# One row of the second weight chunk turned to columns on TensorE instead of through DRAM, and the first even part moved between the two halves of the sine ring's update, with a later conversion of the third weight chunk

## The chip, the cores and the metric

The kernel runs on one core of a Trainium2 chip. The metric is the device time of one execution in microseconds (us). I quote medians over executions with their extremes. The calls ran on different chips (chip 15, 14, 7 and 3), each timed one with the kernel before in the same rounds; medians of different calls are therefore compared with care.

## The reference

```python
def reference(x, w_in, w_out):            # x: 8 x 3008 x 256, w_in: 256 x 2048, w_out: 2048 x 256
    X = np.fft.fft(np.fft.fft(x, axis=1), axis=2).real.astype(np.float32)
    h = X.reshape(-1, 256) @ w_in
    g = np.where(h > 0.0, h, np.exp(np.minimum(h, 0.0)) - 1.0)
    return (g @ w_out).astype(np.float32)
```

The weights arrive as 64-bit floats. The kernel converts them with integer operations, chunk by chunk, while the main work is already running.

## The kernel before

The kernel works in steps, each on 256 sequence positions. The sequence transform gives rings of cosine rows (`Rr`) and sine rows (`Ir`); the channel transform is folded into the first weights, which gives `Wc` and `Ws`. In a step, a cosine product P = `Rr` by `Wc` and a sine product Q = `Ir` by `Ws` are made on TensorE. By symmetry h = E - Q for one half of the positions and E + Q for the other, with the even part E = P + (channel 128) x (its weights).

Channel 128 is the odd one out of 256. Its weights of chunk c are the row 127 of `Ws`, and VectorE needs them as *columns* `wex`, one number for each partition (the cuts of code leave out wrappers, and `...` marks left-out lines):

```python
def even_part(i):
    ...
    for j in range(2):
        f = 2 * (i % 8) + j
        c = slice(j * TW, (j + 1) * TW)
        nc.vector.scalar_tensor_tensor(out=S.E[:, c], in0=Rb[:, cols(i)],
            scalar=wex[:, f : f + 1], in1=S.H[:, c], op0=ALU.mult, op1=ALU.add)

def spread_last_row(q):                      # row 127 of Ws to columns, by way of DRAM
    c = slice(q * 256, (q + 1) * 256)
    queue = nc.sync if q else nc.gpsimd
    queue.dma_start(out=wx_dr[:, c], in_=Ws[127:128, c])
    queue.dma_start(out=wex[:, 2 * q : 2 * q + 2],
                    in_=wx_dr[:, c].rearrange("o (f p) -> p (o f)", p=128))
```

A weight chunk is converted by two masks on VectorE (`fields`), three ScalarE operations (`power`), a GpSimd sum (`round`), and a VectorE sign operation followed by a GpSimd product (`scale`); then TensorE folds it (`fold_chunk`), and ScalarE puts it into `Ws` and `Wc` (`put_chunk`).

The *cosine transform of channel 128 of the later batches* is made at step 25 from an extra input: a gather of single 4-byte elements of x, in sixteen pieces, to SBUF, to DRAM and back in another layout. I call these "the extra channel's rows":

```python
at((13 + 0.7 * n) * T, lambda j=j, k=k: load_ext(j, 192 * k, 192 * (k + 1)))   # n = 0 .. 15
at(24.4 * T, get_ext)                         # read back from DRAM
at(25 * T + 1.35, fold_ext)                   # GpSimd
at(25 * T + 4.75, dft_ext)                    # TensorE
```

`at(t, ...)` puts work at a place in the order of the program; `T` is a step. It sets order, not time.

## Time and profile before

| | us |
|---|---|
| median of the first three runs (lowest, highest) | 1979.97 (1978.64, 1984.95) |
| span of the traced execution | 1978.7 |
| TensorE busy | 1960.0 |
| TensorE waiting for E at Q0, Q1, Q2 | 1.45, 0.84, 4.39 |
| P0 starts; P3 starts; P3 to the end | 27.50; 53.88; 1924.81 |

How to read it: what is not TensorE's own work is found in its waits, and nearly all of them lie in the first 60 us. So three marks are enough: when the first cosine product P0 starts, how long P0 to P3 takes (the stretch that the change touches), and how long P3 to the end takes. The prediction shows the lines themselves.

### The profile page before, as it was taken

The numbers are of one execution on the slowest core, as the hardware profiler recorded it, in microseconds if no ns is written. First come the engines' busy times: TensorE is split into PE (matmuls) and PEld (weight loads), VectorE is DVE, ScalarE is ACT, GpSimd is POOL, SyncE is SP. The second block draws the span as 40 slices with busy tenths as digits, with TensorE's granted clock in tenths as the row PEclk, the third lists the DMA queues.
The fourth block names the chain that finished last, engine by engine and source line by source line (L and its number), as shares of the span: only waits on it lengthen the run. The fifth ranks groups of instructions, "written<-read, shape, count | busy, mean of one in ns | idle before, by whom it ended". The sixth has DMA issues, their size and how long they took to land.

```text
span 1978.7 us, 26821 instructions
## 1 busy us (share of the span) xinstructions
PE 1960.0 (99%) x8896; PEld 1665.0 (84%) x8896; DVE 1273.9 (64%) x2322; ACT 869.4 (44%) x1666; POOL 1333.9 (67%) x1804
## 2 busy tenths in 40 slices
PE   8999999999999999999999999999999999999998
PEld 4888888888888888888888888888888888888887
DVE  7766656666566666666566665666556765666665
ACT  3554434444444444444444443444444444344443
POOL 3388748776577766777567775678657776455655
PEclk9999999999999999999999999999999999999999
DMA  9146201121001110011100211003010110100101
GB/s 355 32 20 45 80 15 19 31 62 22 14 19 43 46 29 12 18 50 41 26 18 13 64 26 26 11 19 89 7 21 12 20 22 14 16 12 12 22 10 23
DMA packets 255740, 71.08 MB, mean 36 GB/s; under 512 B 244255, under 2 KB 245044, under 8 KB 255090
## 3 DMA queue, kind: packets, MB, share of 16 engines
q1 hardware_dynamic: 251026, 56.53, 14.8%
q0 software_dynamic: 2400, 12.59, 1.9%
q8 instruction: 70, 1.15, 0.2%
q14 instruction: 68, 0.56, 0.1%
q10 hardware_dynamic: 2176, 0.26, 0.1%
HBM read 44.50 MB, written 24.80 MB: 35 GB/s over the span
## 4 chain that ended last, share of the span: by engine, by line
PE 96%; DVE 1%; DMA 1%; POOL 1%; issue 0%; ACT 0%; POOLq 0%; DVEq 0%; ACTq 0%
PE H L350 39%; PE pD L350 16%; PE pB L350 16%; PE pC L350 16%; PE pA L350 8%; DMA xl<-in_x_dram,ix 1%; DMA wx<-Ws 0%; DVE E L710 0%; DMA wex<-wx 0%; POOL G L359 0%; DVE v L356 0%; DVE e L423 0%; DVE o L423 0%; DVE Ir L356 0%; DVE G L736 0%
## 5 line engine op out<-in xcount | busy, mean ns | idle before, releaser
L359 POOL TENSOR_TENSOR G<-G 128x256 f32<-128x256 f32 x1440 | 1036.8, 729 | 564.8 <-DVE G L736 453.3
L710 DVE SCALAR_TENSOR_TENSOR E<-Rb,wex,H 128x256 f32<-128x256 f32 x752 | 327.9, 477 | 621.4 <-PE H L350 614.1
L362 ACT ACTIVATE G<-H 128x512 f32<-128x512 f32 x376 | 224.6, 597 | 960.6 <-DVE G L720 960.6
L350 PE MATMUL H<-Ir,Ws 128*128 128x256 f32 x1504 | 388.2, 381 | 6.7 <-DVE E L710 6.7
L350 PE MATMUL H<-Rr,Wc 128*128 128x256 f32 x1504 | 386.4, 379 | 0.0
L350 PE MATMUL pC<-G,WT 128*128 128x256 f32 x1440 | 369.5, 379 | 0.0
L350 PEld LDWEIGHTS H<-Rr,Wc 128*128 128x128 f32 x1504 | 285.1, 190 | 53.8 <-issue 2.5
L350 PEld LDWEIGHTS H<-Ir,Ws 128*128 128x128 f32 x1504 | 278.1, 189 | 56.2 <-DVE E L710 8.9
L350 PEld LDWEIGHTS pC<-G,WT 128*128 128x128 f32 x1440 | 273.6, 190 | 37.2
L720 DVE SCALAR_TENSOR_TENSOR G<-E,H 128x512 f32<-128x512 f32 x376 | 257.3, 684 | 37.5 <-PE H L350 1.9
L736 DVE SCALAR_TENSOR_TENSOR G<-G,H 128x512 f32<-128x512 f32 x376 | 256.0, 681 | 24.9 <-ACT G L362 24.8
L736 DVE SCALAR_TENSOR_TENSOR G<-M,G 128x512 f32<-128x512 f32 x376 | 257.2, 684 | 0.0
L362 ACT ACTIVATE G<-G 128x512 f32<-128x512 f32 x376 | 233.2, 620 | 0.0
L350 PE MATMUL pB<-G,w 128*128 128x256 f32 x784 | 231.0, 382 | 0.0
L350 PE MATMUL pA<-G,w 128*128 128x256 f32 x784 | 229.4, 379 | 0.2 <-POOL w L359 0.2
L350 PE MATMUL pD<-G,w 128*128 128x256 f32 x784 | 229.3, 379 | 0.0
L362 ACT ACTIVATE M<-G 128x512 f32<-128x512 f32 x376 | 224.0, 596 | 0.0
L362 ACT ACTIVATE M<-M 128x512 f32<-128x512 f32 x376 | 221.0, 588 | 0.0
L350 PE MATMUL pD<-G,WT 128*128 128x256 f32 x720 | 214.4, 379 | 1.6 <-DVE v L356 1.6
L350 PE MATMUL pB<-G,WT 128*128 128x256 f32 x720 | 214.5, 379 | 0.5 <-POOL G L359 0.5
L350 PEld LDWEIGHTS pB<-G,w 128*128 128x128 f32 x784 | 150.1, 192 | 20.8
L350 PEld LDWEIGHTS pA<-G,w 128*128 128x128 f32 x784 | 148.9, 190 | 20.8 <-POOL w L359 0.6
(127 smaller groups left out, 1382.9 us busy)
## 6 DMA issues: line engine op xcount, KB each, us to landing
out_dram<-ot SPq DMA_DIRECT2D x496, 32.0 KB
xl<-in_x_dram SPq DMA_DIRECT2D x16, 768.0 KB
MC<-dft_mats SPq DMA_DIRECT2D x4, 1131.0 KB
out_dram<-ot SPq DMA_DIRECT2D x256, 2.0 KB
Rb<-r SPq DMA_DIRECT2D x10, 376.0 KB
raw<-in_moe_w_in_dram SPq DMA_DIRECT2D x7, 512.0 KB
raw<-in_moe_w_out_dram SPq DMA_DIRECT2D x5, 512.0 KB
out_dram<-ot SPq DMA_DIRECT2D x64, 28.0 KB
```

Of the source, the lines that this page charges most:

```text
L350: nc.tensor.matmul(out_, lhsT=lhsT, rhs=rhs, start=start, stop=stop, skip_group_check=True)
L359: pin(nc.gpsimd.tensor_tensor(out=o, in0=a, in1=b, op=op))
L362: pin(nc.scalar.activation(out=o, in_=i, func=func, **kw))
L710: nc.vector.scalar_tensor_tensor(out=S.E[:, c], in0=Rb[:, cols(i)], scalar=wex[:, f : f + 1], in1=S.H[:, c], op0=ALU.mult, op1=ALU.add,)
L720: nc.vector.scalar_tensor_tensor(out=two(S.G[:, 0:512])[:, :, ::-1], in0=two(S.E), scalar=2.0, in1=two(S.H), op0=ALU.mult, op1=ALU.subtract,)
L736: nc.vector.scalar_tensor_tensor(out=o, in0=e, scalar=-1.0, in1=h, op0=ALU.add, op1=ALU.max)
```

## The change

The intent: Q2 waits 4.39 us for two DMA hops of 1 KB. Two TensorE products of one column each can do the same. With a stationary operand of 128 columns of `Ws` and a moving operand that is 1 in row 127 and 0 elsewhere, the product is row 127 as a column. ScalarE copies it to `wex`. Besides, E0 goes between the two updates of the sine ring, and the conversion of chunk 2 moves later, so that VectorE is free for E1.

```diff
-    m = np.zeros((128, 32), np.float32)
+    m = np.zeros((128, 33), np.float32)
     m[np.arange(128), np.arange(128) % 32] = 1.0
+    m[127, 32] = 1.0
...
-    pick = cpool.tile([128, 32], FP, tag="pick")
+    pick = cpool.tile([128, 33], FP, tag="pick")
...
+    def turn_last_row(q):
+        for j in range(2):
+            f = 2 * q + j
+            mm(folds[q][:, j : j + 1], Ws[:, f * 128 : (f + 1) * 128], pick[:, 32:33], True)
+
+    def put_last_row(q):
+        act(wex[:, 2 * q : 2 * q + 2], folds[q][:, 0:2])
...
     w1_chunks[1].load()
+    nc.sync.dma_start(out=pick, in_=PK_dr.ap())
...
-    at(1.2, lambda: nc.sync.dma_start(out=pick, in_=PK_dr.ap()))
...
-        at(t - 0.5 if k else 0.95, chunk.fields)
-        at(t + 0.05 if k else 0.96, chunk.power)
-        at(t + 0.06 if k else 0.97, chunk.round)
-        at(t + 2.95 if k else 1.9, chunk.scale)
+        at(0.96 if k == 0 else t + 3.0 if k == 1 else t - 0.5, chunk.fields)
+        at(0.96 if k == 0 else t + 3.05 if k == 1 else t + 0.05, chunk.power)
+        at(0.97 if k == 0 else t + 3.06 if k == 1 else t + 0.06, chunk.round)
+        at(1.9 if k == 0 else t + 4.22 if k == 1 else t + 2.95, chunk.scale)
...
-        at(t + 0.01, lambda c=c: spread_last_row(c))
+        if c > 1:
+            at(t + 0.01, lambda c=c: spread_last_row(c))
+    at(T + 0.2, lambda: turn_last_row(1))
+    at(T + 0.25, lambda: put_last_row(1))
...
-        (0.1, I_even.minus),
+        (0.95, I_even.minus),
```

(Here k = 1 and 2 are the places of the chunks 2 and 3 of the first weights; k = 0 is the first chunk of the second weights. Chunk 1 was converted before. `pick` is the moving operand of the turn, its column 32 new.)

More of the change, by code (lines that the diff above doesn't have):

```diff
@@ L394, in spread_last_row @@
             )
+    def turn_last_row(q):
+        for j in range(2):
+            f = 2 * q + j
+            mm(
+                folds[q][:, j : j + 1],
+                Ws[:, f * 128 : (f + 1) * 128],
+                pick[:, 32:33],
+                True,
+            )
+    def put_last_row(q):
+        act(wex[:, 2 * q : 2 * q + 2], folds[q][:, 0:2])
     w2v = w2.rearrange("p (q c) -> p q c", c=ND)
@@ L969, in mid_pick @@
         po = state["mo"] = bank("H")
-        mm(po[0:32, 0:ND], pick, state["mh"][:, 0:ND], True)
+        mm(po[0:32, 0:ND], pick[:, 0:32], state["mh"][:, 0:ND], True)
     def mid_store():
```

## The prediction

> **What bounds the kernel now.** I read the page first: busy shares, the chain of waits, the costliest groups. Then the waits of TensorE alone, then the chain in order of time over the first 60 us, and last the timelines of TensorE, VectorE and GpSimd over 27 to 57 us.
>
> ```profile
> PE 1960.0 (99%) x8896; PEld 1665.0 (84%) x8896; DVE 1273.9 (64%) x2322; ACT 869.4 (44%) x1666; POOL 1333.9 (67%) x1804
> PE 96%; DVE 1%; DMA 1%; POOL 1%; issue 0%; ACT 0%; POOLq 0%; DVEq 0%; ACTq 0%
> ```
>
> TensorE sets the time nearly everywhere: 99% busy, 96% of the chain. What is not TensorE's work can only be found in its waits, which are few:
>
> ```profile
> PE H L350 <- DVE E L710: 6.7, 3, 4.4
> PE pD L350 <- DVE v L356: 1.6, 3, 0.5
> PE M L350 <- DVE zero L337: 1.1, 1, 1.1
> PE pC L350 <- DMA MC<-dft_mats: 0.8, 1, 0.8
> PE pB L350 <- POOL G L359: 0.5, 1, 0.5
> ```
>
> The columns are the total in us, the number, and the longest. Three waits of the sine product for the even part E make 6.7 us of some 11. All are early, as TensorE's timeline shows (start, length, work, idle before it):
>
> ```profile
> 29.98 1.10 PE L350 MATMUL H<-Ir,Ws 128*128 128x256 f32 x4 [1.45 <-DVE E L710]
> 36.41 1.13 PE L350 MATMUL H<-Ir,Ws 128*128 128x256 f32 x4 [0.84 <-DVE E L710]
> 40.13 1.89 PE L350 MATMUL pA<-G,w 128*128 128x256 f32 x8
> 46.41 2.07 PE L350 MATMUL H<-Ir,Ws 128*128 128x256 f32 x4 [4.39 <-DVE E L710]
> 48.28 3.62 PE L350 MATMUL pB<-G,w 128*128 128x256 f32 x8
> 51.69 2.36 PE L350 MATMUL H<-w,CC 128*128 128x256 f32 x8
> 53.88 1.03 PE L350 MATMUL H<-Rr,Wc 128*128 128x256 f32 x4
> ```
>
> I call these sine products Q0, Q1, Q2 (step 0, 1, 2), the cosine products before them P0, P1, P2, P3, and the even parts E0, E1, E2. After Q2's wait eight matmuls of 128x256 take 3.62 us; just before it, 1.89. The busy table by stretch shows why, in its clock column (PEclk, before the DMA share): half speed after the wait.
>
> ```profile
> 46.40:51.70 5.30, 5.29 (x13) 4.21 (x14) 4.28 (x7) 2.12 (x4) 1.27 (x1) 0.50 0.47 168
> 54.00:58.00 4.00, 4.00 (x21) 3.51 (x20) 3.05 (x5) 2.35 (x5) 1.30 (x1) 1.00 0.04 3
> ```
>
> What Q2 waited for stands in the chain in order of time: the 1 KB row 127 of Ws, written to DRAM and read back as columns.
>
> ```profile
> 33.25 6.83 DMA wx<-Ws
> 40.09 5.29 DMA wex<-wx
> 45.88 0.49 DVE E L710
> ```
>
> The data is tiny; the hops are long because bulk loads are in flight. The DMA engines are at 90% or more of each slice until about 45 us.
>
> **What the Trainium skill says.** (1) "TensorE: Matmul & The Clock Gate", Part 1: the gate knows half and full speed, falls to half after an idle window of about 3.4 us and needs about as long a busy one to come back. The trace agrees: an idle 4.39 us was followed by clock 0.50 for some 5 us, the idle 1.45 us at Q0 by none. (2) The same page, LDWEIGHTS (loading the stationary operand): a weight load costs by its columns, about 107 ns for 128. The trace differs: its fp32 loads of 128x128 take 190 ns, and a product has two. They are hidden beside matmuls of 256 columns (216 ns from start to start); beside matmuls of one column they are not, so the turn costs its loads. (3) "SBUF — State Buffer", Who interferes with whom: VectorE in a two-port mode, or with two SBUF inputs, and GpSimd exclude each other for a whole instruction. The trace agrees, and this decides my size below: the integer mask ops of a weight chunk take 0.41 us alone and far more beside GpSimd:
>
> ```profile
> 32.98 1.18 DVE L211 TENSOR_SCALAR pow<-raw 128x512 int32<-128x512 int32 x1
> 34.08 1.49 DVE L217 TENSOR_SCALAR w<-raw 128x512 int32<-128x512 int32 x1
> 33.95 1.34 POOL L359 TENSOR_TENSOR w<-w,pow 128x512 f32<-128x512 f32 x1
> ```
>
> The second mask stood right behind the first and still had to let the GpSimd product pass, which had asked earlier. (4) "DMA: Bandwidth & Descriptors", Issuing engines are not separate DMA queues: all issuers share the same 16 engines. It fits the 12 us of the two hops; another queue would not have helped.
>
> **The change part by part.** The built order differs on few places: on TensorE two one-column products (turn) behind P1; on VectorE E0 between the two Ir instructions, chunk 2's masks behind g of step 0, its sign/exponent op behind the two Rr instructions of the odd DFT; on ScalarE one 128x2 copy; two row DMAs gone. GpSimd's order is unchanged. I walk it through with durations of the trace; durations overlap by some 0.08 us on VectorE, so I use starts.
>
> 1. *E0 first.* E0 started 28.96, after both Ir instructions (28.04 and 28.51). Behind the first alone it starts 28.49, ends 29.36, and Q0 goes 0.15 later, 29.52 instead of 29.98. The next work, the fold of chunk 1, needs GpSimd's 29.10 + 1.27 = 30.37, so it starts 30.47 instead of 30.91: gain 0.44. Risk: row 0's columns, by the GpSimd queue, land at 20.98 + 6.6 = 27.6, still 0.9 early.
>
> 2. *The turn.* P1 then ends its turn on TensorE at 30.47 + 1.73 + 0.87 = 33.07. The turn waits for the put of chunk 1 (ScalarE, ends about 33.1): four loads, 4 x 0.19 = 0.76, the following DFT's first load no longer hidden, 0.19, and the wait, 0.07: 1.0 us. The DFT starts 34.1 and Q1 36.0.
>
> 3. *Q1's wait goes.* E1 stood behind the two masks (32.98 to 35.57) and started 35.49. Now it follows h of step 0, needs P1 (33.23), and ends 34.15, long before 36.0. So Q1 comes at 36.0 instead of 36.41: gain so far 0.41. The turn has eaten the 1.0 us (by starts) that this wait gave.
>
> 4. *Q2.* No DMA now: the copy of the columns runs on ScalarE about 35.2. P2 comes at 36.0 + 0.96 + 1.90 = 38.86, the next products take 0.87 + 1.73, so TensorE could start Q2 at 41.46. But E2 stands behind the moved work on VectorE: the odd DFT's Rr pair waits for its matmuls (end 39.0) and ends 40.04; chunk 2's sign op 39.96 to 40.64; chunk 3's first mask 40.56 to 40.97. At 40.64 + 0.15 = 40.8 GpSimd asks for its product of chunk 2, gets the port at 40.97, holds it to about 42.1, and chunk 3's second mask ends at 42.4. E2: 42.33 to 43.2, Q2 at 43.35. The wait shrinks from 4.39 to about 1.8 us, but does not vanish. Gain: 46.41 - 43.35 = 3.06.
>
> 5. *The clock.* A gap of 1.8 us should not drop it. From Q2 to P3 are 20 matmuls: 53.88 - 46.41 = 7.47 us before, 0.87 + 1.73 + 1.73 = 4.33 at full clock: another 3.14.
>
> Sum at P3: 3.06 + 3.14 = 6.2 us (53.88 becomes 47.7). Behind it I find nothing that gives it back: E3 needs P3 and VectorE is free about 48.0; chunk 2's own row now starts at about 48.3, needs two hops on quiet engines, and is used about 55.5; chunk 2's conversion is later by a slot, but its fold at 45.95 needs GpSimd's 42.1. From there TensorE sets the pace at full clock, so the gain is carried whole to the end: 1979.97 - 6.2 = 1973.8.
>
> **The rivals.** (a) *The port is not lost*: chunk 3's second mask takes it at 40.97 ahead of GpSimd. E2 then ends 42.1, Q2 is at 42.25, the gain 7.3: 1972.7. Against it: the 34.08 line above. (b) *The clock falls anyway*, as the DFT, turn and new gap leave TensorE less busy, or as the gap grows past 3 us by further port conflicts: half to all of the 3.14 is lost: 1975.5 to 1977. Against it: 1.45 us idle at Q0 left the clock at 1.00. (c) *A transfer takes the wait over*: the bulk loads are reordered (chunk 2's raw now behind a DFT matrix, the next x earlier); were a later row's columns or row 0's late, some 1 to 3 us would come back. Against it: slacks of about 0.9 us for row 0 and 4 us for row 2. (d) *The end is bound elsewhere*, and the gain is hidden: 1980. Against it: 99% TensorE; GpSimd, at 67%, makes TensorE wait 0.7 us in all.
>
> **Range and chances.** The three runs of before span 1978.6 to 1985.0, as much as the gain, so the median itself may be off by a microsecond or two. With (a) on the one side and (b), (c) on the other, I take 1970.5 to 1977.5. A change over 2% would be 40 us; only 11 us of waits exist, and nothing added is over 1 us: faster 0.5%, slower 1%.
>
> **What would show it.** Right: TensorE's waits for E fall from 6.7 to about 3 us, Q0's wait from 1.45 to about 1.0, Q1's to 0, Q2's to 1.5 to 2 us, released by VectorE's E behind a mask op of over 1 us; clock 1.00 throughout 40 to 54 us; no row DMA before Q2; P3 near 47.7; two one-column products with four loads of 0.19 us. Wrong: a clock of 0.5 after the new gap; E2 released by a DMA; Q2's gap near 0.6 (rival a); or 6 us gained at P3 and missing at 150 us.

## The result, and the profile after

| | before | after |
|---|---|---|
| median of 4 runs (lowest, highest), us | 1981.69 (1978.64, 1984.95) | 1975.37 (1973.97, 1981.91) |
| ratio, 95% interval | | 0.9979 (0.9956 to 1.0003) |
| span of the traced execution, us | 1978.7 | 1974.8 |
| P0 starts, us | 27.50 | 29.03 |
| P0 to P3, us | 26.38 | 19.94 |
| P3 to the end, us | 1924.81 | 1925.86 |

The ratio is the one for runs of the same rounds; it is not the ratio of these medians (0.9968). The time is 1975.37 where 1973.8 was predicted; it lies in the range, but these runs alone do not separate a gain of 0.2% from none.

The busy line and the chain line of the page after:

```profile
PE 1957.2 (99%) x8900; PEld 1663.6 (84%) x8900; DVE 1272.5 (64%) x2322; ACT 869.4 (44%) x1667; POOL 1331.7 (67%) x1804
PE 92%; SPq 2%; DMA 2%; DVE 1%; issue 1%; POOL 1%; ACT 1%; POOLq 0%; DVEq 0%
```

Four more matmuls, one more ScalarE operation, as built. The chain has a new part: the queue of SyncE with 2%, which the chain before did not have, and DMA went from 1% to 2%. TensorE's waits (what, for whom: total us, times, longest) say where it comes from:

```profile
PE H L351 <- DVE E L725: 3.2, 3, 1.7
...
PE pC L351 <- DMA MC<-dft_mats: 1.5, 1, 1.5
PE H L351 <- DMA CC<-chan_mats: 1.2, 1, 1.2
...
PE H L351 <- POOL xe L360: 0.7, 1, 0.7
```

The waits for E fell from 6.7 to 3.2 us, as predicted (the third of them, 0.2 us, stands near 1650 us and is new). But the first loads came later (pC and CC, before P0), and there is a new wait of 0.7 us for `xe`, the extra channel's rows. TensorE's timeline over the stretch of the change (start, length, work, idle before it):

```profile
29.03 1.02 PE L351 MATMUL H<-Rr,Wc 128*128 128x256 f32 x4
31.30 1.10 PE L351 MATMUL H<-Ir,Ws 128*128 128x256 f32 x4 [1.25 <-DVE E L725]
...
34.88 0.61 PE L351 MATMUL H<-pick,Ws 128*128 128x1 f32 x4
...
37.32 1.02 PE L351 MATMUL H<-Ir,Ws 128*128 128x256 f32 x4
...
44.55 1.13 PE L351 MATMUL H<-Ir,Ws 128*128 128x256 f32 x4 [1.71 <-DVE E L725]
...
48.97 1.03 PE L351 MATMUL H<-Rr,Wc 128*128 128x256 f32 x4
```

Q0 waits 1.25, not the 1.0 predicted, because in this execution E0 had to wait for row 0's columns:

```profile
30.28 0.87 DVE L725 SCALAR_TENSOR_TENSOR E<-Rb,wex,H 128x256 f32<-128x256 f32 x2 [0.17 <-DMA wex<-wx]
```

Q1 waits nothing, Q2 1.71 us, and P3 follows Q2 by 4.42 us instead of 7.47. The busy table over that stretch has the clock at 1.00 (the third number from the right), where it was 0.50 before:

```profile
44.50:49.80 5.30, 5.25 (x24) 4.66 (x25) 4.69 (x7) 2.76 (x7) 2.51 (x2) 1.00 0.88 326
```

What Q2 still waits for is what step 4 named. GpSimd's product of chunk 2, then VectorE's second mask of chunk 3 and E2 behind it:

```profile
42.10 1.32 POOL L360 TENSOR_TENSOR w<-w,pow 128x512 f32<-128x512 f32 x1 [0.85 <-DVE pow L255]
```

```profile
42.21 1.50 DVE L218 TENSOR_SCALAR w<-raw 128x512 int32<-128x512 int32 x1
43.63 0.86 DVE L725 SCALAR_TENSOR_TENSOR E<-Rb,wex,H 128x256 f32<-128x256 f32 x2
```

So the traces agree with the prediction up to P3 (6.44 us gained for 6.2), and yet the span differs by 3.9 us only. 1.53 us went before P0 and about 1.05 us behind P3. The question for the experiments: did the change take these back, or are they chance? And how typical is 26.38 for the kernel before?

### The profile page after: what moved, and what is told of

It reads as the page before. It is cut to its first block, busy times and chain, and to the rows that moved or that the text cites. A ratio compares the mean times of both kernels' runs of the same rounds, so it can differ in the third digit from the quotient of the medians.

```text
span 1974.8 us, 26827 instructions
## 1 busy us (share of the span) xinstructions
PE 1957.2 (99%) x8900; PEld 1663.6 (84%) x8900; DVE 1272.5 (64%) x2322; ACT 869.4 (44%) x1667; POOL 1331.7 (67%) x1804
## 4 chain that ended last, share of the span: by engine, by line
PE 92%; SPq 2%; DMA 2%; DVE 1%; issue 1%; POOL 1%; ACT 1%; POOLq 0%; DVEq 0%
PE H L351 38%; PE pD L351 16%; PE pC L351 15%; PE pB L351 15%; PE pA L351 8%; SPq L575 1%; DMA x<-in_x_dram 1%; DVE E L725 0%; DMA wex<-wx 0%; POOL xl L145 0%; SPq L592 0%; DVE v L357 0%; POOL G L360 0%; DVE G L751 0%; POOL w L360 0%
## 5 line engine op out<-in xcount | busy, mean ns | idle before, releaser
L751 DVE SCALAR_TENSOR_TENSOR G<-G,H 128x512 f32<-128x512 f32 x376 | 255.9, 680 | 25.3 <-ACT G L363 25.3
L351 PEld LDWEIGHTS pD<-G,w 128*128 128x128 f32 x784 | 149.0, 190 | 20.2
```

The lines of the kernel that those rows point to most:

```text
L351: nc.tensor.matmul(out_, lhsT=lhsT, rhs=rhs, start=start, stop=stop, skip_group_check=True)
L751: nc.vector.scalar_tensor_tensor(out=o, in0=e, scalar=-1.0, in1=h, op0=ALU.add, op1=ALU.max)
```

## The experiments

The marks of all traces, in us. "Rows" is TensorE's wait for the extra channel's rows; "gather" is the time from the first issue of their gather to the last issue of their reading back. The rows "used later" are explained below.

| kernel | P0 | wait at Q1 | wait at Q2 | P0 to P3 | P0 to P4 | P3 to end | gather | rows |
|---|---|---|---|---|---|---|---|---|
| before | 27.50 | 0.84 | 4.39 | 26.38 | 33.29 | 1924.81 | 50.9 | 0 |
| before, again | 28.02 | 0.85 | 3.77 | 24.25 | 31.15 | 1924.65 | 55.2 | 0 |
| before, third | 27.36 | 0.85 | 3.43 | 25.17 | 32.07 | 1924.99 | 49.9 | 0 |
| before, rows used later | 27.41 | 0.84 | 3.14 | 23.49 | 30.40 | 1925.70 | 51.2 | 0 |
| E0 first alone | 27.30 | 1.24 | 3.44 | 23.84 | 30.75 | 1928.85 | 57.9 | 2.33 |
| after | 29.03 | 0 | 1.71 | 19.94 | 26.84 | 1925.86 | 56.7 | 0.73 |
| after, again | 27.54 | 0 | 1.71 | 19.76 | 26.66 | 1924.97 | 51.2 | 0 |
| after, looks 1 to 3 | 28.49, 27.35, 27.48 | 0 | 1.71 | 19.75, 19.75, 19.76 | 26.66 | 1925.02, 1924.98, 1924.93 | 53.4, 47.7, 51.4 | 0 |
| after, look 4 | 27.45 | 0 | 1.71 | 19.75 | 26.65 | 1935.36 | 64.1 | 8.13 |
| after, rows used later | 27.36, 27.27 | 0 | 1.71 | 19.75 | 26.66 | 1925.59, 1925.53 | 54.7, 54.8 | 0 |
| matrix load late | 27.20 | 0 | 1.71 | 19.75 | 26.66 | 1927.97 | 58.7 | 2.71 |
| turn twice | 27.28 | 0 | 1.71 | 20.20 | 27.11 | 1926.5 | 57.2 | 1.30 |
| conversion not moved | 27.21 | 0.55 | 0 | 18.89 | 25.80 | 1924.6 | 47.7 | 0 |
| masks late (two traces) | 27.13, 27.31 | 0 | 0 | 18.00, 17.99 | 25.57, 25.56 | 1925.58, 1925.48 | 55.2, 47.7 | 0 |
| E2 first | 27.37 | 0 | 0 | 17.78 | 26.02 | 1928.6 | 57.9 | 2.08 |
| masks and fold late | 27.24 | 0 | 0 | 18.00 | 24.91 | 1924.80 | 47.3 | 0 |

### The start: chance, or the earlier load of the small matrix?

The change loads `pick` early (issued at 5.21 us in its first trace, at 27.76 us in the kernel before), ahead of all DFT matrices but the first. The theory (A) was that the late P0 (29.03) is chance of the first x rows, which landed at 15.63 instead of 14.11 us; the rival, that the added early load causes it. Three runs: both kernels unaltered, and the changed one with that load moved back behind the early ones.

Before, unaltered.

> The kernel before, unaltered, for a second trace. Theory A: P0 between 27 and 30 us, not necessarily 27.5; P0 to P3 again 26.4 +- 0.5 us with the 4 us wait for the row's DMA and the half clock. Theory B: P0 again at 27.5 +- 0.3. No wait for the extra channel's rows in either.

Measured: 1978.7 us; P0 28.02, P0 to P3 24.25 us instead of 26.38. The wait at Q2 was 3.77 instead of 4.39, and the slow stretch behind it shorter. The 26.4 +- 0.5 us that both theories took for granted is missed; P0 lies in the range of theory A and outside that of B.

After, unaltered, timed with five rounds.

> The changed kernel once more, unaltered. Between P0 (first cosine product) and P3 its first trace took 48.97 - 29.03 = 19.94 us, the kernel before 53.88 - 27.50 = 26.38: a gain of 6.4, as predicted. But P0 itself came 1.5 us later than before, because the first x rows landed at 15.6 instead of 14.1 us, and a new wait of 0.73 us for the extra channel's rows stood at 181 us. Theory A (chance): how fast the first loads arrive differs from execution to execution; P0 here lies anywhere from 27 to 30, P0 to P3 stays at 19.9 +- 0.3, and the timed gain over before is 4 to 8 us. Theory B (the early load of the pick matrix and the new order of the loads delay the first x rows in every execution): P0 at 29 or later again. The wait at about 181 us (extra channel) appears again at 0.3 to 1.5 us if it is a matter of slack, and not at all if it was chance.

Measured: 1976.02 us (1974.05 to 1980.81; before 1979.68, 1976.22 to 1989.08; ratio 0.9981, 0.9961 to 1.0002). P0 27.54, no wait for the extra channel's rows. The late start and the new wait of the first trace are both gone in the same kernel. The gain between the medians, 3.7 us, is just below the 4 to 8 expected.

The matrix load late, five rounds:

```diff
     w1_chunks[1].load()
-    nc.sync.dma_start(out=pick, in_=PK_dr.ap())
...
         w1_chunks[2].load()
+        nc.sync.dma_start(out=pick, in_=PK_dr.ap())
```

> The changed kernel with the pick matrix loaded behind the second DFT matrix, so that the loads issued in the first 5 us are those of the kernel before. Theory B: P0 back at 27.5 and the time 1.5 us below the changed kernel's. Theory A: P0 anywhere from 27 to 30, the time within 1 us of the changed kernel's. In both the pick matrix lands well before 30 us and the turn does not wait for it; P0 to P3 19.9.

Measured: 1974.16 us (1973.66 to 1976.69), ratio 0.9966 (0.9947 to 0.9984); P0 27.20, a third of a microsecond earlier than in the run before, within the scatter of P0. The median is 1.86 us below that of the run before, which is what theory B expected and outside the 1 us of theory A. But the run before had P0 at 27.54 with the early load, and its runs spread over 6.8 us for another reason (next section); of the twelve timed runs that keep the early load and use the rows later (below), eleven lie within 1.3 us. What follows: the 1.53 us before P0 was chance of the first transfers for the most part. A small cost of the early load is not excluded, since of eight traces of the changed kernel with the early load (two of them with the later use below) two have P0 at 28.49 and 29.03, and of four of the kernel before one at 28.02; the six traces of variants that keep the early load have 27.13 to 27.37. No run separates that. The traced execution of this kernel waited 2.71 us for the extra channel's rows, longer than the changed kernel's first one.

### The extra channel's rows

The theory: that wait is the spread of a slow gather and would come in both kernels; the rival: the change brings it, by starting the gather under heavier DMA load. First the changed kernel with `fold_ext`, `dft_ext` and the work behind them one step later:

```diff
-    at(25 * T + 1.35, fold_ext)
-    at(25 * T + 4.75, dft_ext)
+    at(26 * T + 1.35, fold_ext)
+    at(26 * T + 4.75, dft_ext)
...
+            late = 1 if b == 1 and not kodd else 0
-            at(step * T + 1.0, lambda b=b, kodd=kodd: spread_ext(b, kodd))
+            at((step + late) * T + 1.0, lambda b=b, kodd=kodd: spread_ext(b, kodd))
```

> The changed kernel with the extra channel's fold, DFT and the first spread of its rows one step (4.8 us) later. If the wait of 0.73 us at 181 us is short slack of the transfers that bring the channel's rows, it is gone, and from P3 to the end the trace takes as long as before (1978.7 - 53.88 = 1924.8 us) or less, instead of 1974.8 - 48.97 = 1925.8 in the changed kernel; timed 0.5 to 1 us faster than the changed kernel. Rival: the lost microsecond sits elsewhere, and P3 to the end stays at 1925.8.

Measured: 1974.6 us (1974.39 to 1976.98), ratio 0.997 (0.9951 to 0.9989). The wait for the rows is gone, and with it most of the spread; a new wait of 0.68 us appeared near 203 us, where the moved work meets the next batch's transform. So P3 to the end is 1925.59 us, and the 1924.8 or less that was expected is missed by about that wait.

Then four more looks at the unaltered changed kernel, to catch one of its long executions (up to 1981.91 us) in a trace.

> The changed kernel again, one of four more looks, to see where its executions differ by 8 us (1974.0 to 1981.9). P0 to P3 should be 19.7 to 20.0 us in each. Theory S (start): a longer run comes late to P0, because a first load lands late, and shows it there. Theory X (extra channel): it waits 2 to 6 us for the extra channel's rows near 180 us. Theory C (clock): neither, but a lower clock somewhere behind a new gap of over 3 us. A run of 1974 to 1976 should have P0 near 27.3 us and at most 0.7 us of that wait.

> As the look before it: P0 to P3 19.7 to 20.0 us, and the time above 1974 us explained by the start (P0 later than 27.3 us), by the wait for the extra channel's rows, or by the clock.

> As the look before it: P0 to P3 19.7 to 20.0 us, and the time above 1974 us explained by the start (P0 later than 27.3 us), by the wait for the extra channel's rows, or by the clock.

> As the look before it: P0 to P3 19.7 to 20.0 us, and the time above 1974 us explained by the start (P0 later than 27.3 us), by the wait for the extra channel's rows, or by the clock.

Measured: 1975.03, 1973.85, 1973.95 and 1984.34 us. P0 to P3 was 19.75 or 19.76 in all four. The fourth is a long one, and its waits show why; this is the first line of TensorE's waits, and the place in its timeline:

```profile
PE H L351 <- POOL xe L360: 8.1, 1, 8.1
```

```profile
186.53 4.17 PE L351 MATMUL H<-MC,xe 128*8 128x377 f32 x24 [8.13 <-POOL xe L360]
```

The 24 products take 4.17 us instead of 2.09, at a granted clock of 0.83 over 170 to 200 us: the clock fell after the gap of 8 us, and so one late transfer is paid twice (8.13 + 2.08 of the 10.4 us that P3 to the end is longer than in the other looks). The delay is seen in SyncE's queue. Of look 2, which did not wait, the first eight pieces of the gather and the last issue of reading back:

```profile
118.22 15.20 SPq L575 DMA_DIRECT2D x<-in_x_dram  x8
...
165.91 0.36 SPq L598 DMA_DIRECT2D xs<-xe_dr  x1
```

and the same of look 4:

```profile
118.29 19.88 SPq L575 DMA_DIRECT2D x<-in_x_dram  x8
...
182.41 0.36 SPq L598 DMA_DIRECT2D xs<-xe_dr  x1
```

The same kernel, the same start, and 64.1 us instead of 47.7 for it. Heavier traffic of this core does not show: from 125 to 165 us its DMA engines moved 2 to 11 GB/s in look 2 and 2 to 5 in look 4. Why the same small transfers take longer stays open. From the first issue to the moment when GpSimd is free for the fold are 57.1 us in every trace of both kernels (62.4 or 62.5 with the later use). Hence TensorE waits when the gather takes over some 56 us, whichever kernel it is: "E0 first alone", which is the kernel before with one event moved and no turn, waited 2.33 us at a gather of 57.9. No trace of the unaltered kernel before shows the wait.

Last, the same later use in *both* kernels, in the same rounds on the same chip.

> The kernel before with the extra channel's fold, products and first rows one step later, so that its rows have 62.5 instead of 57.1 us to arrive. Theory: the long executions of the kernel before are those rows too; its highest time falls from 1985 to 1989 to some 1982, its median stays within 1 us of 1979 (0.7 us lost to a meeting with the next batch's work, as in the changed kernel with the same edit). Rival: the long ones have another cause and stay.

> The changed kernel with the same edit, on the same chip in the same rounds. Theory: with the late rows taken out of both, the change shows what the traces give it at P3, 19.8 against 24 to 26.4 us: 4.5 to 6 us between the medians, and none of its runs over 1978. Rival: the difference stays at 3.7 us or less, and something between P3 and the end gives some of it back.

Measured: before 1979.09 us (1976.97 to 1982.45), after 1974.46 us (1974.23 to 1975.52). The means of the six runs each are 1979.20 and 1974.66: 4.5 us, a ratio of 0.9977. The changed kernel's spread has shrunk from 6.8 us (with five rounds) to 1.3 us; that of before is 5.5 us (six runs) where the unaltered one has 10.0 (eleven runs, up to 1986.63). With "E0 first alone" this says that an order without the turn has this tail too, so the change does not bring it. Whether it makes the wait more frequent is not excluded: with the rows at their old place one of four traces without the turn waits, and five of thirteen with it. The rival, that something behind P3 gives back part of the gain, falls: P3 to the end is 1925.70 and 1925.53 us.

Part of what remains of before's spread is its own Q2 (P0 to P3 is 23.49 to 26.38 us in four traces; its longest run, 1982.45, has no trace). The trace of before with the later use, Q2 and the products behind it, and the third trace of before:

```profile
45.05 2.07 PE L350 MATMUL H<-Ir,Ws 128*128 128x256 f32 x4 [3.14 <-DVE E L710]
46.92 2.42 PE L350 MATMUL pB<-G,w 128*128 128x256 f32 x8
```

```profile
45.32 2.08 PE L350 MATMUL H<-Ir,Ws 128*128 128x256 f32 x4 [3.43 <-DVE E L710]
47.19 3.62 PE L350 MATMUL pB<-G,w 128*128 128x256 f32 x8
```

That third trace:

> The kernel before, unaltered, a third trace. Theory: Q2's wait follows how long the two row transfers take beside the bulk loads, and what the clock takes back follows by how far that wait reaches over the idle window; so P0 to P3 comes out anywhere from 24 to 26.5 us, and the first trace's 26.38 was at the upper end. Rival: 26.4 is the typical figure and the second trace's 24.25 the exception: 26 to 26.7.

Measured: 1979.29 us, P0 to P3 25.17 us. The two fences show the clock's part: waits of nearly one length, but the eight products behind take 2.42 us in one (part of them at full speed) and 3.62 in the other. "E0 first alone" below waits 3.44 us, and its eight take 2.45. So the part of the theory by which the loss follows the length of the wait fails. The rival, that 26.4 is typical, falls.

### E0 first alone

```diff
-        (0.1, I_even.minus),
+        (0.92, I_even.minus),
```

on the kernel before, nothing else.

> The kernel before with only E0 moved ahead of the second Ir instruction, nothing else. My step 1 gave this 0.44 us. Theory: Q0 comes 0.2 to 0.5 us earlier after P0, but Q2 still waits 3.5 to 4.5 us for the row's columns from DRAM and the clock still falls behind it, so P0 to P3 is 24 to 26 us as in the kernel before: alone the part is worth 0 to 0.4 us, which a timing cannot show. Rival: E0 is what brings the gain, and P0 to P3 is near 20.

Measured: 1981.79 us, P0 to P3 23.84, and the wait of 2.33 us for the rows. TensorE's timeline, Q0, Q1, Q2:

```profile
29.39 1.10 PE L350 MATMUL H<-Ir,Ws 128*128 128x256 f32 x4 [1.06 <-DVE E L710]
...
36.21 1.13 PE L350 MATMUL H<-Ir,Ws 128*128 128x256 f32 x4 [1.24 <-DVE E L710]
...
45.27 2.08 PE L350 MATMUL H<-Ir,Ws 128*128 128x256 f32 x4 [3.44 <-DVE E L710]
```

Q0 comes 2.09 us after P0, before 2.48: the predicted 0.4 us. (P0 to P3 and the wait at Q2 are a little under the 24 to 26 and 3.5 to 4.5 us expected.) But Q1 comes 8.91 us after P0, exactly as in the kernel before (36.41 - 27.50): its wait grew from 0.84 to 1.24. Alone, the part is worth nothing, because E1 stands behind the masks. Whether it pays beside the move of the conversion, which frees Q1, no run separates.

### The turn, doubled

```diff
     at(T + 0.2, lambda: turn_last_row(1))
+    at(T + 0.21, lambda: turn_last_row(1))
```

> The changed kernel with the turn made twice (the same result). The prediction counted 1.0 us for a turn; the trace shows 0.51 us between P1's usual end and the DFT. If a turn costs 0.5 us, the DFT starts 0.87 + 2 x 0.5 = 1.9 us after P1 and Q1, Q2 and P3 all come 0.4 to 0.5 us later (P3 at 20.2 from P0); if the loads are not hidden at all, 0.76 us or more and P3 at 20.5.

Measured: 1975.77 us; P0 to P4 27.11 against 26.66 us: 0.45 us for one more turn. In the changed kernel's own trace, P1 to the following DFT is 35.34 - 33.96 = 1.38 us against 0.87 before: 0.51 us, half of what step 2 gave it. The weight loads show why:

```profile
34.87 0.52 PEld L351 LDWEIGHTS H<-pick,Ws 128*128 128x128 f32 x4 [0.29 <-ACT Wc L363]
```

Four loads in 0.52 us are 0.13 us each, not 0.19.

### The port behind Q2's remaining wait

Theory P: Q2 still waits because chunk 3's second mask loses the shared port to GpSimd's product of chunk 2, and E2 stands behind it. The rival: E2 is late for another reason (P2, or VectorE simply full), so that moving the masks shifts the wait but does not remove it. First, the masks of chunk 3 behind E2:

```diff
-        at(... else t - 0.5, chunk.fields)
+        at(... else t + 0.95 if k == 2 else t - 0.5, chunk.fields)
         (chunk.power and chunk.round with it, at t + 1.0 and t + 1.01)
```

> The changed kernel with chunk 3's two mask ops behind E2 instead of ahead of it. In the changed kernel (second trace, times from P0) Q2 comes at 15.34 after a wait of 1.71 us and P3 at 19.76. Theory P (port): E2 is late because chunk 3's second mask waits for GpSimd's product of chunk 2; with the masks behind it E2 follows chunk 2's sign op, Q2 comes at about 13.9 with a wait of 0.3 to 0.5 us and P3 at 18.3. Rival (E2 waits for P2 or for the Rr pair): the wait stays over 1.2 us and P3 at 19.2 or later.

Measured: 1972.51 us; no wait at Q2, P0 to P3 18.00 us. VectorE's timeline:

```profile
39.79 0.86 DVE L725 SCALAR_TENSOR_TENSOR E<-Rb,wex,H 128x256 f32<-128x256 f32 x2
40.57 1.00 DVE L212 TENSOR_SCALAR pow<-raw 128x512 int32<-128x512 int32 x1
41.49 0.41 DVE L218 TENSOR_SCALAR w<-raw 128x512 int32<-128x512 int32 x1
```

The mask still meets GpSimd (1.00 us), but now nobody waits for it. One step later 0.40 us is lost at Q3, where a fold of x and a mask are blocked by the next GpSimd operations. Of the 1.75 us to P3, 1.1 us is left at P4. Theory P holds; it gave 0.3 to 0.5 us of wait at Q2, and there is none.

Then also chunk 2's sign operation behind E2, five rounds:

```diff
-        at(... t + 4.22 if k == 1 else t + 2.95, chunk.scale)
+        at(... t + T + 0.93 if k == 1 else t + 2.95, chunk.scale)
```

> As masks_late, and chunk 2's sign op also behind E2. Theory P: E2 follows the Rr pair at once, Q2 needs no wait over 0.1 us (13.5 from P0), P3 at 17.8 from P0, 1.9 us earlier than in the changed kernel, and the time falls by 1 to 2.5 us against it: about 1973 us median. Rival: the gain is given back at the folds of chunks 2 and 3, whose GpSimd products come up to 2 us later, and P3 or the step behind it shows a new wait for GpSimd.

Measured: 1973.88 us (1973.06 to 1975.54), ratio 0.9969 (0.9955 to 0.9982). Q2 is without a wait again, but Q3 waits 1.06 us: between E2 and E3 three VectorE operations (a mask, the moved sign operation and the x fold) took 1.50, 1.46 and 1.70 us, where the same ones take 0.4, 0.7 and 0.9 us undisturbed. P0 to P4 is 26.02 us, so two thirds of the gain at P3 are given back one step on: the rival in this expectation came true in part.

The conversion of chunk 2 where the kernel before has it (turn and early E0 kept):

> The changed kernel with chunk 2's conversion left where the kernel before has it (ahead of E1); the turn and the early E0 stay. Theory P: E1 again stands behind two masks held up by GpSimd, so Q1 waits 0.4 to 0.9 us (8.9 from P0 instead of 8.12), but chunk 2's GpSimd product is then over before chunk 3's masks, so these take 0.41 us each and Q2 comes at about 14.7 with a wait under 0.6 us; P3 at 19.1 +- 0.3 from P0: the move of the conversion gains nothing, it costs about 0.6 us. Rival (the move pays, as the prediction had it for Q1): P3 at 20.3 or later.

Measured: 1972.48 us. Q1 waits 0.55 us again, Q2 not at all; P0 to P4 25.80 us, 0.86 less than the changed kernel. The move of the conversion, which freed Q1, costs more at Q2 than it brings. This order also differs from "E0 first alone" by little but the turn and its matrix's load: P0 to P3 is 18.89 against 23.84 us, so the turn is what brings the gain, about 5 us in this pair of traces.

The late masks again, now timed with five rounds:

> The changed kernel with chunk 3's masks behind E2, now timed. The look at it showed Q2 without a wait and P0 to P3 18.00 us instead of 19.8, with 0.40 us given back at Q3. Theory P (the GpSimd port decided what was left of Q2's wait): the same marks again, P0 to P4 25.6 us, 1.1 us less than the changed kernel's 26.7, and a median near 1973 to 1974.5. Rival: the look was a lucky execution and the 1.1 us does not show: P0 to P4 near 26.7, a median of 1975 to 1976.

Measured: 1973.99 us (1972.58 to 1981.81), ratio 0.9981 (0.9963 to 1.0); P0 to P4 25.56 us, the same marks as in the look.

Last, the late masks and the x fold `EO3`, which only step 4 needs, behind E3:

```diff
-    at(2 * T + 4.2, lambda: fold_now("EO3"))
+    at(3 * T + 1.0, lambda: fold_now("EO3"))
```

> As the last, and the x fold that the odd cosine part needs only in step 4 moved behind E3, so that E3 is no longer behind it. Theory P: Q3's 0.40 us wait goes, P0 to P4 25.1 to 25.3 us, so some 0.4 us less than the kernel with the late masks alone; a median of 1972.5 to 1974. Rival: the fold now meets GpSimd between E3 and g and makes a later sine or even part late: a new wait of 0.3 to 1 us at step 4 and no gain.

Measured: 1972.12 us (1971.81 to 1981.72; before 1979.39, 1977.57 to 1983.49), ratio 0.9971 (0.9951 to 0.999). P0 to P4 24.91 us, and neither Q2 nor Q3 waits:

```profile
40.82 1.13 PE L351 MATMUL H<-Ir,Ws 128*128 128x256 f32 x4
...
47.83 1.03 PE L351 MATMUL H<-Ir,Ws 128*128 128x256 f32 x4
```

It has the lowest median of all kernels here, under what was expected (1972.5 to 1974; P0 to P4 25.1 to 25.3): 7.3 us below the kernel before in the same rounds. Its one run at 1981.72 has no trace; the extra channel's rows would explain it, but that is not shown for this run.

## Why the prediction was right or wrong

**Step 1, E0 first (0.44 us).** Right in size where the trace is undisturbed: Q0 comes 2.08 us after P0 in five of the six traces of the unaltered changed kernel, against 2.48 before. In the first one it was 2.27, as row 0's columns came 0.2 us late. What the prediction didn't say: alone the part brings nothing.

**Step 2, the turn (1.0 us).** Mis-sized: 0.51 us, and 0.45 for a second one. The term that failed is "four loads, 4 x 0.19": it took the duration of loads that lie beside long matmuls. With one-column products between them, four loads took 0.52 us together. The 0.19 us for the following DFT's first load did not show either: from the turn's start to the DFT's are 35.34 - 34.88 = 0.46 us.

**Step 3, Q1's wait goes.** Right. As the turn is cheaper, Q1 comes 8.12 us after P0 instead of the 8.5 worked out. But the move that frees Q1 was a net loss: with the conversion left in its place P0 to P4 is 0.86 us shorter.

**Step 4, the remaining wait at Q2 (about 1.8 us), by the port.** Right: 1.71 us in all ten traces with the changed order on VectorE, released by E behind a mask of 1.50 us, and gone when the masks are moved. Rival (a), the port not lost, did not happen. (The 1.75 us of the late masks are no measure of it, as in (a) the masks stay ahead of E2.)

**Step 5, the clock (3.14 us).** The mechanism is right: the clock is 1.00 after a gap of 1.71 us, and rival (b) falls. The size was taken from one trace of the kernel before. From Q2 to P3 the four traces of the kernel before take 7.47, 5.97, 7.21 and 5.85 us, where the changed kernel takes 4.42: 3.05, 1.55, 2.79 and 1.43 us, 2.2 on average. So the term is 2.2, not 3.14. It does not follow the length of the gap (in this order 4.39, 3.77, 3.43, 3.14).

**The sum (6.2 us at P3).** 6.44 us in the pair that was predicted from. But over the four traces of before, P0 to P3 is 24.8 us on average, and the changed kernel's typical figure is 19.75: 5.1 us, of which 2.9 come up to Q2 and 2.2 behind it. That 6.44 lies so near to 6.2 is in part luck: the turn was taken 0.5 us too dear, and row 0's late columns took 0.2 of that back. The kernel before is not one number, as its Q2 waits for a transfer among others; the changed one nearly is.

**"Behind it I find nothing that gives it back ... carried whole to the end".** In executions without the extra channel's wait this holds to 0.2 us on average: P3 to the end is 1924.65 to 1924.99 before and 1924.93 to 1925.02 after. A new wait of 0.2 us for E near 1650 us goes with it, in every trace of the changed kernel with the rows at their old place and in none of before; its cause was not looked for. The step that failed is this last one, the base of the sum and its carrying to the end, 1979.97 - 6.2 = 1973.8. It took the executions for equal but for a shift, and the first trace for typical. It left out a wait that was 0 in the trace that I read: that for the extra channel's rows, which was 0.73 and 8.13 us in two of the six traces of the changed kernel, and 2.33 in "E0 first alone". And of the terms of the sum it is the clock's that was mis-sized most (2.2 for 3.14, step 5). The pair with later rows gives 4.5 us for the change, the plain pair of five rounds 3.7 us between medians, where 6.2 was predicted. The number 1973.8 itself is that of an undisturbed execution (1973.85 and 1973.95 in looks 2 and 3); the median of 1975.37 has in it the first trace (1976.6), with its late start and its wait, and a run of 1981.91 that has no trace.

**Rival (c), a transfer takes the wait over.** It came true in small: in the first trace row 0's columns landed at 30.14 us instead of 27.6, and Q0 came 0.2 us late by it; in the five other traces of the kernel they did not hold E0 up. The larger wait is that of a transfer which (c) did not name. **Rival (d)** did not happen.

One small misreading in the prediction: the DMA engines are at 90% or more of each slice from 3 us on, not from the start.

Open: why the gather takes longer in some executions and whether the change makes that more frequent, whether the early load of `pick` delays the start by a fraction of a microsecond, and the untraced long executions of the other kernels.

## What to carry to other kernels

A tiny transfer that is needed soon, while bulk loads run, can be slow and differ from execution to execution: here the first hop of 1 KB took 6.83 us beside them, and the same hop of chunk 2's row 1.2 us on quiet engines. Moving it to an engine gained its mean wait and the clock's loss, and took the spread of this stretch away. Once such a wait was gone, the next one stood close behind it: look at who shares VectorE's port with GpSimd just ahead of the operation that the bound engine waits for, and move what nobody waits for behind it. Before a gain of some microseconds is predicted or judged, take several traces of the kernel before, and list the waits that are zero in one and large in another.

## What the Trainium skill lacked or had wrong

- "TensorE: Matmul & The Clock Gate", Part 1 names an idle window of about 3.4 us before the clock falls, free-running. Here a gap of 3.14 us already dropped it (0.72 on average over the next 5.3 us), 1.71 us never did. The section "Why this matters for your kernels", which advises gaps of no more than about 3 us, fits better (the ends of matmuls in a trace are modelled). The loss after one gap was 1.4 to 3.1 us and did not follow the gap's length, which fits the free-running window.
- The same page, "LDWEIGHTS (loading the stationary operand)": one figure by columns, about 107 ns for 128. Here fp32 loads of 128x128 took 190 ns beside matmuls of 256 columns, and 0.13 us each (four in 0.52 us) between one-column products. That the cost depends on what lies beside it is not said there.
- "DMA: Bandwidth & Descriptors" has no figure for a gather of single 4-byte elements, nor for its spread. Here the same gather with its reading back took 47.3 to 64.1 us in 20 traces.
